# The softmax sum's small constant and broadcast move to GpSimd, and the 64-bit weight conversion takes its sign in ScalarE's pass

## The chip, the cores and the metric

The kernel runs on one core of one Trainium2 chip. The metric is the device time in microseconds (us) of one execution. The engines of the core work side by side: TensorE (PE in the profile, with its weight loads as PEld), VectorE (DVE), ScalarE (ACT), GpSimd (POOL) and SyncE (SP, which only issues transfers here).

## The reference

An attention with a bias from a small network, followed by two feed-forward stages on 2304 tokens. Cut to what matters:

```
scores = q @ k.T / 8 + bias            # 4 batches, 8 heads, 576 positions, 64 wide
attn   = exp(scores - max)
attn   = attn / (sum(attn) + 1e-9)
x      = attn @ v                      # 2304 tokens x 512
h      = x @ w_in                      # 512 -> 2048; w_in, w_out are 64-bit floats
g      = (a0 + a1 h + a2 h^2 + a3 h^3) / (1 + |b0||h| + |b1| h^2 + 1e-6)
y      = g @ w_out                     # 2048 -> 512
out    = max(y @ w1, y @ w2, y @ w3) @ w_out2   # 512 -> 768 -> 512; these weights are 64-bit too
```

## The kernel before

The kernel has three stages. In **attention** it walks over 80 units; a unit is one batch b, one tile t of 128 query rows (t = 4 is the tail of 64) and one pair p of heads, and five units (t = 0 to 4) make a block of one batch and pair. For a unit, `scores` multiplies q and k on TensorE, `reduce_min` adds the bias on VectorE and finds each row's maximum (L258), `expo` takes the exponential and its row sum on ScalarE (L264, sum into `st`), `normalise` forms the inverse sum and spreads it over 128 columns (`rb`, L269 to L272), and `transposes` turns the exponentials and `rb` on TensorE (L296, L302, L303; L303 reads `rb`). `attn_v` multiplies with v and `attn_store` applies the turned inverse sum. The transposes of a unit come two units after its scores. GpSimd splits q and k of coming pairs into a high and a low part (L138 to L153).

The **first feed-forward stage** has five blocks of tokens with 16 steps each. A step is twelve matmuls into `ph` (L459), a chain of six VectorE and five ScalarE instructions on it (`rat_poly`, `rat_inv`, `rat_newton`, L480 to L496), a split of the result `gs` by ScalarE and GpSimd (L506, L507), and two steps later twelve matmuls into `y`. The **second stage** does likewise with three products `p` and their maximum.

The weights lie in memory as 64-bit floats. `weight_stages` turns one block of 128 x 512 of them into 32-bit floats: ScalarE scales the high words (L382), VectorE shifts the low words (L383), shifts the high words and joins both (L388), takes the sign bit from the high word (L396), and then ScalarE and GpSimd split the result (L412, L413; in some blocks VectorE does L413). There are 56 such blocks: 16 of w_in during attention (`wrwin`, written back as 32-bit floats `wi_n`), 16 of the first w_out around the end of attention and the first block of feed-forward (`wrwo`), and 24 of the second stage (`wrm`, `wrmo`), of which one starts with each of the 16 steps of the last feed-forward block and the rest follow in the second stage. Three buffers (`raw`) hold the loaded words; a load waits until an earlier block has left its buffer.

SyncE follows the program's own order throughout. TensorE does too from the ninth unit to the last, and in feed-forward TensorE and VectorE do, once the last units have drained. Elsewhere a scheduler sets an engine's order when the kernel is built; on GpSimd and ScalarE it does so everywhere. Each engine carries out its list strictly in order: an instruction that has to wait holds up all behind it.

Of the kernel before, what the change touches and what calls it, by code (L numbers as in the profile page):

```python
# [12 lines left out]
AF = mybir.ActivationFunctionType  # L13
ALU = mybir.AluOpType
# [3 lines left out]
P = 128  # L18
# [10 lines left out]
TW = 1148  # L29
KN = {'NSLOT': 35, 'NRAW': 3, 'NRAWX': 2, 'NATT': 4, 'HB': 0, 'NE': 'd', 'FP': 2, 'BL': 4, 'T4': 0, 'LSP': 1, 'KX': 4, 'HT': 'ss', 'EVP': 'da', 'TTP': 'dda', 'NXS': 4, 'EARLY': 0, 'NM0': 8, 'MAN': 2, 'MANF': 3, 'A1': ['b', 'T', 'sc', 'st', 'r0', 'av', 'b', 'b', 'b', 'sq', 'n', 'r1', 'p2', 'v0', 'v1', 'e0', 'e1'], 'A2': ['sc', 'av', 'p1', 'T', 'r1', 'r0', 'n', 'st', 'p2', 'sq', 'e0', 'e1', 'v0', 'v1'], 'LL': 10, 'SL': 4, 'LL0': 9, 'SL0': 4, 'SQ': [2, 1, 1], 'CUT2': 2, 'CUT3': 3, 'WS': 9, 'WE': 70, 'WT': 61, 'XT': 8, 'XA': 3, 'XB': 8, 'F': ['g2a', 'g2d', 'h', 'g1a', 'w', 'g2p', 'g1d', 'g1p', 'y', 'x', 'g3'], 'LOW': 4, 'LOM': 3, 'LOI': 0, 'GHI': 'dve', 'GLO': 'dve', 'BED': 8, 'BE0': 16, 'NU1': 'pool', 'XE': ['act', 'pool'], 'WR': 1, 'YSP': 'act', 'LAG': 2, 'EV1': 'dve', 'XSE': 'act', 'STQ': 'sp', 'PUQ': 'sp', 'NB0': 0, 'HP': 0, 'SB': 2, 'XLA': 3, 'XLB': 6, 'XSA': 11, 'YL': 10, 'YS': 14, 'WLOW': 1}  # L30
REBIAS = 2.0 ** -112
SIGN = -(1 << 31)
QC = 1.0 + 1e-6
NSMALL = 76 + S // 4

# [2 lines left out]
def tile_attention_moe(  # L38
# [7 lines left out]
    pe, act, dve, pool, sp = nc.tensor, nc.scalar, nc.vector, nc.gpsimd, nc.sync  # L46
# [8 lines left out]
    def raw(name, shape, dt):  # L55
        return sb.tile(shape, dt, tag="raw", name=name, bufs=KN['NRAW'])
# [16 lines left out]
    def f32(ap):  # L73
        return ap.bitcast(F32)
# [11 lines left out]
    parts = (slice(TOFF - 124, TW), slice(0, TOFF - 124))  # L86
# [179 lines left out]
    def normalise(b, t, p):  # L266
        et, st = ex[b, t, p]
        r = st[:, 2:4] if t < 4 else st[:, 2:3]
        dve.tensor_scalar(r, r, 1e-9, None, ALU.add)  # L269
        rb = sb.tile([P, 2, 64], F32, tag="rb", name=f"rb{b}_{t}_{p}", bufs=4)  # L270
        dve.reciprocal(r, r)
        evac(KN["NE"], (rb, r.unsqueeze(2).to_broadcast([P, 2, 64])))  # L272
        rbs[b, t, p] = rb
        if t == 4:
            pool.tensor_copy(et[:, 1, :64], et[:, 0, 512:])
# [37 lines left out]
    def evac(e, pair):  # L313
        if e == "a":
            act.copy(*pair)
        elif e == "d":
            dve.tensor_copy(*pair)  # L317
        else:
            pool.tensor_copy(*pair)
# [32 lines left out]
    def weight_place(name, n, packed):  # L352
        if packed and len(spare) == 8:
            parts = [[spare[4 * a + k] for k in range(4)] for a in range(2)]
            spare.clear()
            wt_[name, n] = parts
            return
        wt = slot(f"w{name}{n}", [P, 9, P], F32R)
        if packed:
            spare.append(wt[:, 8])  # L360
        wt_[name, n] = wt
# [5 lines left out]
    def weight_stages(src, name, n, packed=False, lo_eng=pool, narrow=None):  # L367
        box = {}
        wide_ = src.dtype != F32

        def load():
            if wide_:
                box["r"] = raw(f"wr{name}{n}", [P, 512, 2], I32)
                sp.dma_start(box["r"], src[n].bitcast(I32).rearrange("p (c w) -> p c w", w=2))
            else:
                box["r"] = raw(f"wr{name}{n}", [P, 512], F32)
                sp.dma_start(box["r"], src[n])

        def rebias():
            if wide_:  # L380
                low, high = box["r"][:, :, 0], box["r"][:, :, 1]
                act.activation(f32(high), f32(high), AF.Copy, scale=REBIAS)  # L382
                dve.tensor_scalar(low, low, 29, None, ALU.logical_shift_right)  # L383

        def join():
            if wide_:
                low, high = box["r"][:, :, 0], box["r"][:, :, 1]
                dve.scalar_tensor_tensor(low, high, 3, low, ALU.logical_shift_left, ALU.bitwise_or)  # L388

        def sign():  # L390
            if wide_:
                low, high = box["r"][:, :, 0], box["r"][:, :, 1]
                res = low
                if narrow is not None:
                    res = sb.tile([P, 512], I32, tag="xs", name=f"wn{name}{n}", bufs=KN['NXS'])
                dve.scalar_tensor_tensor(res, high, SIGN, low, ALU.bitwise_and, ALU.bitwise_or)  # L396
                box["r"] = f32(res)

        def put():
            (act if KN["PUQ"] == "act" else sp).dma_start(narrow[n], box["r"])  # L400

        def parts():
            weight_place(name, n, packed)
            r, w = box["r"], wt_[name, n]
            if isinstance(w, list):
                for k in range(4):
                    act.copy(w[0][k], r[:, k * P:(k + 1) * P])
                for k in range(4):
                    lo_eng.tensor_tensor(w[1][k], r[:, k * P:(k + 1) * P], f32(w[0][k]), ALU.subtract)
            else:  # L410
                hi, lo = (w[:, 4 * a:4 * a + 4].rearrange("p k c -> p (k c)") for a in range(2))
                act.copy(hi, r)  # L412
                lo_eng.tensor_tensor(lo, r, f32(hi), ALU.subtract)  # L413

        if narrow is not None:
            return [load, rebias, join, lambda: (sign(), put())]
        return [load, rebias, lambda: (join(), sign()), parts]

    pipe, todo = [], []

    def weights_tick(new=1):
        for st in list(pipe):
            st.pop(0)()
            if not st:
                pipe.remove(st)
        for _ in range(new):
            if todo:
                st = weight_stages(*todo.pop(0))
                st.pop(0)()
                pipe.append(st)  # L430
# [195 lines left out]
    early = []  # L626
    if wi.dtype != F32:
        for nm, src, cnt in (("wi", wi, NF), ("wo", wo, KN['EARLY'])):
            slim[nm] = dr.tile([NF, P, 512], F32, tag=f"{nm}_n", name=f"{nm}_n")
            early += [weight_stages(src, nm + "n", f, narrow=slim[nm]) for f in range(cnt)]  # L630
    eq = [st[0] for st in early[:2]]
    for i, st in enumerate(early):
        eq += st[1:3] + [st[0] for st in early[i + 2:i + 3]] + st[3:]
    n_early = len(eq)

    def low_eng(m, f):
# [82 lines left out]
    def attn_tick(n):  # L719
# [11 lines left out]
        for step in KN["A1" if n < KN["NM0"] else "A2"]:  # L731
# [13 lines left out]
            elif step == "n" and u1:  # L745
                normalise(u1[0], u1[2], u1[3])
            elif step == "v0" and u2:
                act.copy(*ev[0])  # L748
            elif step == "v1" and u2:
                for e_ in ev[1:len(ev) - 1]:  # L750
                    evac(KN["EVP"][n % len(KN["EVP"])], e_)
                evac(KN["TTP"][n % len(KN["TTP"])], ev[-1])
            elif step == "b":
                bias_step()
            elif step in ("p1", "p2"):
                early_pop(n, 0.5 * int(step[1]))
            elif step == "av":
                if avq:
                    av, js = avq.pop(0)
                    attn_v(*av, js)  # L760
                    if 4 in js:
                        stq.append(av)
                if u2 and u2[2] == u2[1][-1]:
                    av = (u2[0], u2[1], u2[3])
                    cuts = {1: (5,), 2: (3, 2), 3: (2, 2, 1)}
                    cut = {1: (5,), 2: cuts[KN["CUT2"]], 3: cuts[KN["CUT3"]]}[len(u2[1])]
                    avq.extend((av, range(sum(cut[:k]), sum(cut[:k + 1]))) for k in range(len(cut)))
            elif step == "sq":
                for bp in splits_at.get(n, []):
                    sqq.extend(split_kq(*bp))  # L770
                for _ in range(2 if n < 10 else KN["SQ"][n % len(KN["SQ"])]):
                    if sqq:
                        sqq.pop(0)()
# [121 lines left out]
```

## Time and profile before

| what | before |
|---|---|
| median of 3 runs | 1100.29 us (1100.19 to 1100.94) |
| the profiled execution, its own time | 1100.39 us |
| its span, first to last instruction | 1098.6 us |
| busy: TensorE, VectorE, ScalarE, GpSimd | 1040.5, 750.8, 620.7, 418.9 us |
| mean granted TensorE clock | 0.985 of full speed |

Attention ends about 363 us into the span, the first feed-forward stage lies from there to about 805 us, and the second fills the rest. A busy TensorE is not one at its peak, since its records overlap; how fast it goes is read from the distance between the starts of equal groups of matmuls.

### The profile page before, as it was taken

The numbers are of one execution on the slowest core, as the hardware profiler recorded it, in microseconds if no ns is written. First come the engines' busy times: TensorE is split into PE (matmuls) and PEld (weight loads), VectorE is DVE, ScalarE is ACT, GpSimd is POOL, SyncE is SP. The second block draws the span as 40 slices with busy tenths as digits, with TensorE's granted clock in tenths as the row PEclk, the third lists the DMA queues.
The fourth block names the chain that finished last, engine by engine and source line by source line (L and its number), as shares of the span: only waits on it lengthen the run. The fifth ranks groups of instructions, "written<-read, shape, count | busy, mean of one in ns | idle before, by whom it ended". The sixth has DMA issues, their size and how long they took to land. (4 is left out here: it accounts for less than half of the span.)

```text
span 1098.6 us, 16477 instructions
## 1 busy us (share of the span) xinstructions
PE 1040.5 (95%) x5996; PEld 811.5 (74%) x5996; DVE 750.8 (68%) x1512; ACT 620.7 (57%) x1226; POOL 418.9 (38%) x409
## 2 busy tenths in 40 slices
PE   5699999999999879999999999999999999999998
PEld 2247677677776557878889788777688788888887
DVE  8496899899998899877789777799984211111111
ACT  5686667676778667766678766777632211211111
POOL 7614555455486534322233323243442330211111
PEclk9799999999999889999999999999999999999999
DMA  7486845255455422010020200223233200201010
GB/s 261 158 314 217 291 153 168 99 204 173 155 160 174 136 103 77 1 58 1 1 77 1 78 1 1 78 77 115 77 118 131 77 1 1 77 1 58 1 39 20
DMA packets 43393, 107.94 MB, mean 98 GB/s; under 512 B 4784, under 2 KB 11184, under 8 KB 43312
## 3 DMA queue, kind: packets, MB, share of 16 engines
q1 hardware_dynamic: 38128, 96.27, 26.1%
q10 hardware_dynamic: 5184, 10.62, 2.5%
q8 instruction: 47, 0.77, 0.3%
q14 instruction: 34, 0.28, 0.1%
HBM read 77.90 MB, written 28.97 MB: 97 GB/s over the span
## 5 line engine op out<-in xcount | busy, mean ns | idle before, releaser
L459 PE MATMUL p<-ys,wm 128*128 128x512 f32 (+1 forms) x1080 | 228.8, 369 | 2.8 <-POOL wm L413 1.8
L459 PE MATMUL ph<-xs,wwi 128*128 128x512 f32 (+1 forms) x960 | 217.8, 375 | 5.7 <-ACT at L748 3.5
L459 PEld LDWEIGHTS p<-ys,wm 128*128 128x128 f32 x1080 | 188.4, 188 | 39.4 <-POOL wm L413 2.2
L459 PE MATMUL y<-gs,wwo 128*128 128x512 f32 (+1 forms) x905 | 207.7, 374 | 7.9 <-POOL gs L507 7.2
L459 PEld LDWEIGHTS ph<-xs,wwi 128*128 128x128 f32 x960 | 170.4, 191 | 41.8 <-POOL xs L451 3.8
L507 POOL TENSOR_TENSOR gs<-g,gs 128x512 fp32r<-128x512 f32 (+1 forms) x80 | 102.2, 1277 | 234.6 <-ACT gs L506 160.2
L459 PEld LDWEIGHTS y<-gs,wwo 128*128 128x128 f32 x905 | 157.3, 188 | 46.4 <-POOL gs L507 13.7
L264 ACT ACTIVATE e<-e,st 128x576 f32<-128x576 f32 x144 | 111.5, 775 | 59.3 <-DVE st L258 53.4
L551 POOL TENSOR_TENSOR h2s<-mx,h2s 128x512 fp32r<-128x512 f32 (+1 forms) x30 | 35.9, 1197 | 226.9 <-ACT h2s L550 226.9
L258 DVE CUSTOM_DVE_ANT_0 e<-s,bias 128x576 f32<-128x576 f32 x144 | 104.0, 751 | 16.3 <-PE s L233 11.7
L547 DVE TENSOR_TENSOR mx<-p,mx 128x512 f32<-128x512 f32 (+1 forms) x30 | 19.1, 637 | 140.0 <-PE p L459 136.1
L480 ACT ACTIVATE s<-ph,keep 128x512 f32<-128x512 f32 (+1 forms) x80 | 49.3, 617 | 75.9 <-PE ph L459 74.1
L233 PE MATMUL s<-k,qs 128*128 128x288 f32 x512 | 86.3, 308 | 4.6 <-DVE st L258 2.8
L550 ACT CAST h2s<-mx 128x512 fp32r<-128x512 f32 (+1 forms) x30 | 17.3, 578 | 128.9 <-DVE mx L548 128.9
L296 PEld LDWEIGHTS tp<-ident,e 128*128 128x128 f32 x576 | 62.5, 142 | 35.6 <-issue 17.1
L296 PE MATMUL tp<-ident,e 128*128 128x128 f32 x576 | 82.0, 282 | 1.0 <-DVE at L317 0.8
L482 DVE SCALAR_TENSOR_TENSOR g<-g,keep,s 128x512 f32<-128x512 f32 (+1 forms) x80 | 55.2, 690 | 36.6 <-ACT g L481 36.0
L338 PE MATMUL av<-at,v 128*64 128x320 f32 (+3 forms) x576 | 77.7, 392 | 1.3 <-DVE st L269 0.7
L565 PE MATMUL o<-wmo,h2s 128*128 128x512 f32 x324 | 78.6, 390 | 0.0
L233 PEld LDWEIGHTS s<-k,qs 128*128 128x128 f32 x512 | 70.6, 189 | 9.0 <-DVE st L258 3.7
L185 PE MATMUL pb<-h,keep 128*32 128x288 f32 x576 | 48.7, 442 | 23.8 <-ACT h L173 22.6
L487 ACT ACTIVATE s<-g,keep 128x512 f32<-128x512 f32 (+1 forms) x80 | 52.7, 659 | 31.7 <-DVE g L482 31.6
(102 smaller groups left out, 1665.0 us busy)
## 6 DMA issues: line engine op xcount, KB each, us to landing
bias_d<-bo ACTq DMA_DIRECT2D x36, 288.0 KB, 2.9
kr<-in_k SPq DMA_DIRECT2D x16, 576.0 KB, 5.1
qr<-in_q SPq DMA_DIRECT2D x16, 576.0 KB, 5.6
bias<-bias_d SPq DMA_DIRECT2D x16, 576.0 KB, 5.3
wrm<-in_m SPq DMA_DIRECT2D x18, 512.0 KB, 3.6
wrwin<-in_wi SPq DMA_DIRECT2D x16, 512.0 KB, 4.4
wrwo<-in_wo SPq DMA_DIRECT2D x16, 512.0 KB, 3.7
v<-in_v SPq DMA_DIRECT2D x8, 576.0 KB, 4.5
```

The lines of the kernel that those rows point to most:

```text
L185: pe.matmul(pb[32 * c:32 * c + 32, x, :HS], lhsT=hw_sb, rhs=hs[c][:, x * HS:(x + 1) * HS], start=True, stop=True,)
L233: pe.matmul(pt[:, x, :HS], lhsT=qs[:, u, t * P:(t + 1) * P], rhs=ks[u][:, w, x * HS:(x + 1) * HS], start=w == 0, stop=w == 1,)
L258: dve.tensor_tensor_reduce(out=dst, in0=src, in1=bs, op0=ALU.add, op1=ALU.min, scale=-0.125, scalar=3.0e38, accum_out=st[:, u:u + 1],)
L264: act.activation(et[:, u], et[:, u], AF.Exp, bias=st[:, u:u + 1], scale=-1.0, accum_out=st[:, 2 + u:3 + u])
L296: pe.transpose(tp[:, j * P:(j + 1) * P], flat[:, 640 * u + j * P:640 * u + (j + 1) * P], ident)
L338: pe.matmul(po[r, :n], lhsT=l, rhs=m, start=j == 0, stop=j == 4, skip_group_check=True)
L459: pe.matmul(po, lhsT=wpart(key, a, k), rhs=rhs, start=first and i == 0, stop=last and i == 2)
L480: act.activation(s, ph, AF.Abs, scale=B0)
L482: dve.scalar_tensor_tensor(q, q, B1, s, ALU.mult, ALU.add)
L487: act.activation(s, q, AF.Ln, bias=qcol)
L507: pool.tensor_tensor(t[1], u, f32(t[0]), ALU.subtract)
L565: pe.matmul(po, lhsT=h[:, a, tt * P:(tt + 1) * P], rhs=w[c], start=j == 0 and i == 0, stop=j == NF2 - 1 and i == 2,)
```

## The change

It has two parts. In `normalise`, adding 1e-9 and spreading the inverse over `rb` are now GpSimd instructions; the reciprocal between them stays on VectorE. In `weight_stages`, ScalarE's pass over the high words is a ReLU with a slope of -2^32 for negative inputs in place of a plain scaling, so that a negative number leaves a mark which the shift in `join` moves into the sign's place; the separate VectorE pass for the sign is gone. The list of early stages is adjusted to three stages in place of four.

```
-SIGN = -(1 << 31)
+TOSIGN = -2.0 ** 32
...
     def normalise(b, t, p):
         et, st = ex[b, t, p]
         r = st[:, 2:4] if t < 4 else st[:, 2:3]
-        dve.tensor_scalar(r, r, 1e-9, None, ALU.add)
+        pool.tensor_scalar(r, r, 1e-9, 0.0, ALU.add, ALU.add)
+        dve.reciprocal(r, r)
         rb = sb.tile([P, 2, 64], F32, tag="rb", name=f"rb{b}_{t}_{p}", bufs=4)
-        dve.reciprocal(r, r)
-        evac(KN["NE"], (rb, r.unsqueeze(2).to_broadcast([P, 2, 64])))
+        pool.tensor_copy(rb, r.unsqueeze(2).to_broadcast([P, 2, 64]))
...
         def rebias():
-                act.activation(f32(high), f32(high), AF.Copy, scale=REBIAS)
+                act.activation(f32(high), f32(high), AF.Prelu, scale=REBIAS, alpha=TOSIGN)
                 dve.tensor_scalar(low, low, 29, None, ALU.logical_shift_right)
...
         def join():
-            if wide_:
-                low, high = box["r"][:, :, 0], box["r"][:, :, 1]
-                dve.scalar_tensor_tensor(low, high, 3, low, ALU.logical_shift_left, ALU.bitwise_or)
-
-        def sign():
             if wide_:
...
-                dve.scalar_tensor_tensor(res, high, SIGN, low, ALU.bitwise_and, ALU.bitwise_or)
+                dve.scalar_tensor_tensor(res, high, 3, low, ALU.logical_shift_left, ALU.bitwise_or)
...
-            return [load, rebias, join, lambda: (sign(), put())]
-        return [load, rebias, lambda: (join(), sign()), parts]
+            return [load, rebias, lambda: (join(), put())]
+        return [load, rebias, join, parts]
...
-        eq += st[1:3] + [st[0] for st in early[i + 2:i + 3]] + st[3:]
+        eq += st[1:2] + [st[0] for st in early[i + 2:i + 3]] + st[2:]
```

Order before, on GpSimd, in the third batch where the queries and keys of a coming pair are split (`qs`, `k`) while the first pair's last unit (`e_4_0`) ends:

```order
L138 TENSOR_SCALAR qs_2_2909<-qr_2_2687 128x1024
L144 TENSOR_SCALAR k_2_0_2910<-kr_2_2685 128x576
L141 TENSOR_TENSOR qs_2_2909<-qr_2_2687,qs_2_2909 64x512 x2
L275 COPY e_4_0_2872<-e_4_0_2872 128x64
L147 TENSOR_TENSOR k_2_0_2910<-kr_2_2685,k_2_0_2910 128x576
L144 TENSOR_SCALAR k_2_1_2911<-kr_2_2685 128x576
L147 TENSOR_TENSOR k_2_1_2911<-kr_2_2685,k_2_1_2911 128x576
```

And the same place with the change, where `st` is the row sum (L269 adds the constant) and `rb` the spread inverse (L272), of units t = 3, 4 and 0:

```order
L138 TENSOR_SCALAR qs_2_2900<-qr_2_2679 128x1024
L144 TENSOR_SCALAR k_2_0_2901<-kr_2_2677 128x576
L272 COPY rb_3_0_2892<-st_3_0_2822 128x128
L141 TENSOR_TENSOR qs_2_2900<-qr_2_2679,qs_2_2900 64x512 x2
L269 TENSOR_SCALAR st_4_0_2864<-st_4_0_2864 128x1
L275 COPY e_4_0_2863<-e_4_0_2863 128x64
L147 TENSOR_TENSOR k_2_0_2901<-kr_2_2677,k_2_0_2901 128x576
L144 TENSOR_SCALAR k_2_1_2902<-kr_2_2677 128x576
L269 TENSOR_SCALAR st_0_1_2916<-st_0_1_2916 128x2
L272 COPY rb_4_0_2951<-st_4_0_2864 128x128
L147 TENSOR_TENSOR k_2_1_2902<-kr_2_2677,k_2_1_2902 128x576
L272 COPY rb_0_1_2992<-st_0_1_2916 128x128
```

The additions and copies now stand between the splits, and `st_4_0` stands behind both L141.

On VectorE the reciprocal of that unit stands, with the change, behind the next unit's two bias passes (L258) and ahead of the evacuation and the bias passes that follow:

```order
L258 ISA e_0_1_2915,st_0_1_2916<-s_0_1_0_2917,bias_1_273 128x576
L258 ISA st_0_1_2916 128x1
L270 RECIPROCAL st_4_0_2864<-st_4_0_2864 128x1
L383 TENSOR_SCALAR wrwin_2663<-wrwin_2663 128x512
L317 COPY att_2_0_2772<-tt_3_0_2944 128x2x128
L258 ISA e_1_1_2964,st_1_1_2965<-s_1_1_1_2971,bias_1_432 128x576
```

Before, the addition stood at that place, the reciprocal and the copy behind it; what follows now waits there for GpSimd.

Order before, on VectorE, in the last feed-forward block, from the last instruction of one step's chain (L496) to the first of the next (L482), in a step in which VectorE also splits a weight block (L413):

```order
L496 SCALAR_TENSOR_TENSOR g_4_7874<-s_4_7873,g_4_7874 128x512
L413 TENSOR_TENSOR wm_7890<-wrm_7744,wm_7890 128x512
L388 SCALAR_TENSOR_TENSOR wrmo_7795<-wrmo_7795 128x512
L396 SCALAR_TENSOR_TENSOR wrmo_7795<-wrmo_7795 128x512
L383 TENSOR_SCALAR wrm_7846<-wrm_7846 128x512
L482 SCALAR_TENSOR_TENSOR g_5_7925<-g_5_7925,keep,s_5_7924 128x512
```

With the change (line numbers are lower by 5 there):

```order
L491 SCALAR_TENSOR_TENSOR g_4_7839<-s_4_7838,g_4_7839 128x512
L408 TENSOR_TENSOR wm_7855<-wrm_7711,wm_7855 128x512
L391 SCALAR_TENSOR_TENSOR wrmo_7761<-wrmo_7761 128x512
L383 TENSOR_SCALAR wrm_7811<-wrm_7811 128x512
L477 SCALAR_TENSOR_TENSOR g_5_7889<-g_5_7889,keep,s_5_7888 128x512
```

One of three conversion passes of the step is gone, and nothing else has moved.

## Rows read from the trace of the kernel before

**Rows 1.** The page's first part: busy us (share of the span) and instructions.

```profile
PE 1040.5 (95%) x5996; PEld 811.5 (74%) x5996; DVE 750.8 (68%) x1512; ACT 620.7 (57%) x1226; POOL 418.9 (38%) x409
```

**Rows 2.** Timeline of TensorE: start us, us, engine, line; first scores of four blocks.

```profile
124.48 1.30 PE L233 MATMUL s<-k,qs 128*128 128x288 f32 x8
...
217.01 1.30 PE L233 MATMUL s<-k,qs 128*128 128x288 f32 x8
...
234.05 1.30 PE L233 MATMUL s<-k,qs 128*128 128x288 f32 x8
...
336.75 1.30 PE L233 MATMUL s<-k,qs 128*128 128x288 f32 x8
```

**Rows 3.** Busy time by stretch, two of attention: length, PE, PEld, DVE, ACT, POOL.

```profile
217.00:234.00 17.00, 17.00 (x128) 12.64 (x127) 15.49 (x44) 12.53 (x30) 9.82 (x12) 1.00 0.59 207
...
319.00:336.00 17.00, 17.00 (x128) 12.64 (x127) 15.44 (x45) 14.42 (x37) 16.22 (x19) 1.00 0.44 126
```

**Rows 4.** VectorE's groups by form, 124 to 354 us: busy us, mean ns.

```profile
L317 DVE COPY rb<-st 128x128 f32<-128x128 f32 x65 | 30.4, 468 | 2.2
L269 DVE TENSOR_SCALAR st<-st 128x2 f32<-128x2 f32 x52 | 20.3, 391 | 0.2 <-ACT e L264 0.2
...
L269 DVE TENSOR_SCALAR st<-st 128x1 f32<-128x1 f32 x13 | 1.9, 147 | 0.0
```

**Rows 5.** Timeline of all engines around 190 us (in brackets: idle before, and releaser).

```profile
189.92 2.52 POOL L141 TENSOR_TENSOR qs<-qr,qs 64x512 fp32r<-64x512 f32 x2
...
190.10 1.18 DVE L317 COPY rb<-st 128x128 f32<-128x128 f32 x1
...
193.64 0.33 PE L302 MATMUL tt<-ident,e 128*128 128x128 f32 x1 [1.19 <-DVE at L317]
```

**Rows 6.** Two GpSimd groups: one line (ns min/median/max), and by form, 124 to 354 us.

```profile
L275 POOL COPY e<-e x16: 227/238/786, 103.8 to 354.4; 128x64 f32<-128x64 f32 x16
...
L138 POOL TENSOR_SCALAR qs<-qr 128x1024 fp32r<-128x1024 f32 x11 | 11.5, 1050 | 1.0
```

**Rows 7.** Timeline of VectorE, second bias pass of a unit that opens a block.

```profile
237.14 0.75 DVE L258 CUSTOM_DVE_ANT_0 e<-s,bias 128x576 f32<-128x576 f32 x1
```

**Rows 8.** Timeline of TensorE after attention, and one stretch's busy times (seventh value: granted clock).

```profile
367.24 5.49 PE L459 MATMUL ph<-xs,wwi 128*128 128x512 f32 x12 [3.48 <-ACT at L748]
...
389.30 1.22 PE L459 MATMUL y<-gs,wwi 128*128 128x512 f32 x2 [4.78 <-ACT gs L506]
390.32 4.56 PE L459 MATMUL ph<-xs,wwi 128*128 128x512 f32 x12
...
367.24:372.66 5.42, 5.42 (x12) 3.80 (x12) 5.36 (x10) 3.29 (x6) 0.00 (x0) 0.50 0.66 236
```

**Rows 9.** Timeline of the last feed-forward block, VectorE and then TensorE.

```profile
733.38 0.73 DVE L482 SCALAR_TENSOR_TENSOR g<-g,keep,s 128x512 f32<-128x512 f32 x1
...
738.31 0.69 DVE L396 SCALAR_TENSOR_TENSOR wrm<-wrm 128x512 int32<-128x512 int32 x1
738.92 0.42 DVE L383 TENSOR_SCALAR wrm<-wrm 128x512 int32<-128x512 int32 x1
...
752.72 0.73 DVE L482 SCALAR_TENSOR_TENSOR g<-g,keep,s 128x512 f32<-128x512 f32 x1
...
708.63 2.90 PE L459 MATMUL ph<-xs,wwi 128*128 128x512 f32 x12
...
736.26 2.90 PE L459 MATMUL ph<-xs,wwi 128*128 128x512 f32 x12
...
787.79 0.98 PE L459 MATMUL p<-ys,wm 128*128 128x512 f32 x2
```

**Rows 10.** Waits over the whole span: us in total, times, longest.

```profile
PE y L459 <- POOL gs L507: 7.2, 10, 1.2
```

**Rows 11.** ScalarE's groups by form: busy us, mean ns.

```profile
L382 ACT ACTIVATE wrm<-wrm 128x512 f32<-128x512 f32 x18 | 12.2, 679 | 15.7 <-DMA wrm<-in_m 15.7
...
L79 ACT ACT_TABLE_LOAD x1 | 1.3, 1283 | 0.7 <-PEq L885 0.7
```

## The prediction, written before the changed kernel ran

> **What bounds the kernel now.** I read the page's first part, then TensorE's starts in its timeline, then the waits that break its pace. TensorE is busy for 95% of the span, VectorE for 68%, ScalarE for 57% and GpSimd for 38% [rows 1]. Such shares are means over stages, so the pace comes first. In attention a block of five units takes 17.04 us where nothing disturbs it (217.01 to 234.05), with TensorE busy for 17.00 of 17 us [rows 2, 3]. From 124.48 to 336.75 twelve blocks take 212.27 us, and twelve at 17.04 would take 204.48 [rows 2]. So 7.8 us is all that any other engine costs there, although VectorE is busy for 15.49 of 17 us [rows 3]. The largest gain that the change can bring to attention is therefore 7.8 us, not the VectorE time that it removes.
>
> What breaks the pace in attention can be seen at 190 us. GpSimd runs two splits of q for 2.52 us, VectorE's small copy into `rb` beside them takes 1.18 us, and TensorE then waits 1.19 us for a VectorE evacuation that came late [rows 5]. The mean tells the same: that copy takes 468 ns, and the addition of 1e-9 takes 391 ns for two columns, but 147 ns for one [rows 4]. VectorE loses time to GpSimd in the very instructions that the change takes from it.
>
> After attention TensorE stands longest: 3.48 us behind a ScalarE copy, and 4.78 us behind the split of the first `gs`. Behind both waits twelve matmuls take 5.49 and 4.56 us in place of 2.90, at a granted clock of 0.50, which is 1.2 GHz, the lower of its two levels [rows 8, 9]. These three rows hold 3.48 + 4.78 + 2.59 + 1.66 = 12.5 us.
>
> In the last feed-forward block five steps took 27.63 us (708.63 to 736.26, so 5.53 a step), but the next eight took 51.53, against 44.21 at that pace: 7.3 us lost [rows 9]. VectorE sets that pace: three of its steps take 19.34 us (733.38 to 752.72), and TensorE needs 16.58 for three [rows 9].
>
> **The sign pass.** It leaves 56 times. In the last feed-forward block its place in the row is 0.61 us (738.31 to 738.92) [rows 9]. Three steps of VectorE shrink from 19.34 to 17.5 us, still 0.9 above TensorE's 16.58. Before, VectorE had fallen 3.5 us behind from 708 to 739 before TensorE waited for over a microsecond; with 0.3 us to spare in ordinary steps, it now falls behind only in each third step, the one in which it splits a weight block too, and by about 4 us in all four such rounds. I therefore leave TensorE a loss of 1.3 us and take a gain of **6** out of 7.3 (ends 5 and 7.3). In the first feed-forward block the conversions of w_out stand in the same row; TensorE's waits of `y` for `gs` are 7.2 us in all, most of them in the last block [rows 10]. I take **1** for the first block (ends 0 and 2).
>
> At the end of attention the scheduler still orders VectorE and puts conversions of w_out ahead of the first `g`. ScalarE's next copy waits for the sign pass, and TensorE for ScalarE. About eleven conversions lie there, so VectorE sheds 11 x 0.61 to 0.69, some 7 us. But the loads of w_out wait for three buffers, so a part of this only moves the stall to the load that is late next. The ends are 0 (the loads set everything) and 12.5 (both waits and the slow clock behind them go). I take **5**: about 1.5 us off each wait, and half of the 4.2 us at the lower clock.
>
> ScalarE's new pass does not stand in the trace. The nearest row is the pass that it replaces, 679 ns for the same 128x512 [rows 11]; I take the same. Its bounds are that and twice that, which would be 38 us more on an engine that idles for 43% of the span [rows 1], so nothing in the sum. Where the cover is gone, in the conversions after attention, the upper end would take back 0.7 us a conversion, which the lower end of that term covers.
>
> **The addition and the copy.** VectorE loses 30.4 + 20.3 + 1.9 = 52.6 us over 65 units, 4 us a block [rows 4], and falls from 15.5 to 11.4 of 17 us even before the sign passes. Its late evacuations should go, and with them most of the 7.8 us; I take **6** (ends 0 and 7.8).
>
> GpSimd gains two instructions a unit. A copy of 128x64 takes 0.238 us and a pass over 128x1024 takes 1.05, so 0.85 ns a column, and the copy of 128x128 is estimated at 0.29 [rows 6]. The trace has no GpSimd pass over two columns in these rows; it lies between 0 and 0.238, and I take 0.15. Together that is 0.44 us a unit, 2.2 a block. In an ordinary block 9.82 + 2.2 = 12 of 17 us fit. From 319 to 336 us, where splits of k, q and w_in meet, GpSimd is busy for 16.22 of 17 us already [rows 3], and 18.4 don't fit.
>
> The order adds a wait as well. The reciprocal now waits on VectorE for GpSimd's addition, and the next unit's evacuation and bias passes are queued behind it; ScalarE's exponentials and TensorE's scores wait for those. For t = 4 the addition stands behind `rb` of t = 3 and both L141: 0.29 + 2.52 + 0.15 = 3.0 us from one reciprocal to the next, against a unit of 17.04 / 5 = 3.41. So it just fits, and VectorE has its two bias passes to do meanwhile (0.75 each [rows 7]). From 319 to 336 us two weight splits stand between as well, and it doesn't fit. I charge **3.5** there: 1.4 of overload, and 2.1 for VectorE held behind a reciprocal (ends 0 and 8).
>
> A rule speaks against this part. The Trainium skill, GPSIMD Engine Reference, section Engine selection, recommends VectorE for elementwise work and puts GpSimd at about half its speed for two inputs, near line rate for one. At half VectorE's speed I estimate the pair at 0.8 us, which still fits the ordinary block by 0.1 us, adds 1.8 us to the overload and would make the sum 1088. The row of 0.238 us for 64 columns on GpSimd supports the faster reading.
>
> **The sum.** Against the profiled execution's 1100.39 us (span 1098.6, and 1.8 around it; the median of the runs is 1100.29): minus 6 (last block), 1 (first block), 5 (after attention) and 6 (attention), plus 3.5 (GpSimd), so minus 14.5: **1086 us**. The second stage and the start get nothing: the second stage runs on TensorE's pace, and at the start the additions only change engine.
>
> **Rivals.** *GpSimd becomes what TensorE waits for* (slower). A pair on GpSimd could cost more than 0.44 us, since it also waits for VectorE: the copy of 128x64 took up to 0.786 [rows 6]. At 2 x 0.79 = 1.58 us each of 13 blocks loses 1.58 + 2.52 - 3.41 = 0.7, the stretch at 319 us loses 16.22 + 7.9 - 17 = 7, and attention's 6 don't come: 1100.4 - 12 + 9 + 7 = 1104. It decides from about 1.35 us a pair on, where the loss eats the 12. For it speaks that GpSimd is full at 319 us; against it that VectorE issues fewer of the instructions that collide. The Trainium skill, SBUF — State Buffer, section Who interferes with whom, calls the pair of ports that both share an exclusive lock, held for the whole instruction; the trace agrees with its 1.18 us for the small copy [rows 5].
>
> *The gain after attention comes in full.* If the two waits shrink enough for the clock to stay at 2.4 GHz, 12.5 come in place of 5, and with attention's whole 7.8: about 1077. For it speaks that the lower clock appears right behind the long waits; against it the loads.
>
> *Nothing comes of it.* The loads set the pace after attention (0), attention's gain and GpSimd's loss cancel, and the last block's VectorE time returns as a wait of GpSimd's splits, whose instructions stand in the same chain: 1099 to 1101. Against it speaks that VectorE has no idle time between the steps of that block.
>
> *The new function needs another table.* Two loads a conversion at 1.283 us [rows 11] are 144 us on ScalarE, and a time well above 1110. The program of the change holds a single load, at the start, as before.
>
> **Chances.** The forecast, 1079 to 1094 by itself, gets 0.66; the full gain (1070 to 1079) 0.14; nothing 0.09; slower 0.11, the table in it. A difference under 0.2%, 2.2 us, can't be told from none here. So faster 0.80, same 0.09, slower 0.11. The range reaches from the full gain, 1072, to a gain that just shows, 1098.
>
> **What would show it.** Right: three steps near 17.5 us on VectorE in the last block and a TensorE period near 5.6; blocks of attention at 17.04 with no wait for `at` or `st` on VectorE; waits shorter than 3.48 and 4.78 after attention; GpSimd's copy near 0.29 us. Wrong: TensorE waiting for `rb`, VectorE idle ahead of reciprocals for more than a few microseconds in all, ScalarE's pass above 0.7 us, or blocks above 17.04 all through attention.

## The result, and the profile after

The changed kernel takes 1085.25 us (median of 4 runs, 1084.40 to 1086.93) against 1100.42 for the kernel before on the same chip: a ratio of 0.9863, 95% interval 0.9846 to 0.9880. The prediction was 1086.0. The profiled execution spans 1083.2 us against 1098.6, so 15.4 us less. The total was met; several of the terms were not, and that their misses cancelled was luck.

The page's first part after the change, busy us by engine, answers to [rows 1]: VectorE is shed of 93.1 us, and GpSimd takes on 33.8.

```profile
PE 1034.7 (96%) x5996; PEld 814.2 (75%) x5996; DVE 657.7 (61%) x1296; ACT 622.8 (57%) x1226; POOL 452.7 (42%) x569
```

To see where the time went I cut each span at starts that TensorE's timeline shows: the turning of `rb` (L303) of the 14th, 64th, 74th and 80th unit, the first `ph` of the second and of the last feed-forward block, the first `p`, the first `o`, and the end. "Steady attention" is the stretch from the 14th to the 64th unit. Lengths in us, from one profiled execution each:

| kernel | units to 14 | steady attention | to unit 74 | to unit 80 | first FFN block | blocks 2 to 4 | last block | to first `o` | rest |
|---|---|---|---|---|---|---|---|---|---|
| before | 128.19 | 177.71 | 34.57 | 23.01 | 101.88 | 225.83 | 96.60 | 24.78 | 286.03 |
| after | 132.24 | 170.68 | 43.25 | 21.09 | 95.07 | 225.85 | 89.28 | 21.95 | 283.79 |
| difference | +4.1 | -7.0 | +8.7 | -1.9 | -6.8 | 0 | -7.3 | -2.8 | -2.2 |

The one great loss lies in the fourth column, around 325 us, where splits of k, q and w_in meet. Busy times by stretch, as in [rows 3], of an ordinary block and of this place (the seventh value is the granted clock):

```profile
217.00:234.00 17.00, 17.00 (x128) 12.64 (x126) 13.14 (x35) 12.33 (x30) 12.46 (x23) 1.00 0.52 178
...
317.00:334.00 17.00, 12.32 (x80) 8.82 (x78) 7.13 (x23) 10.47 (x28) 15.42 (x24) 0.83 0.44 136
```

In the ordinary block TensorE has no gap, and GpSimd went from 9.82 to 12.46 of 17 us. At 317 us GpSimd is the busiest engine with 15.42, TensorE stands for 4.7, and the granted clock falls to 0.83 on average. The timeline says why. First VectorE's reciprocal of a unit with t = 4, then GpSimd's row, then TensorE:

```profile
323.83 0.16 DVE L270 RECIPROCAL st<-st 128x1 f32<-128x1 f32 x1 [2.94 <-POOL st L269]
...
323.56 0.23 POOL L269 TENSOR_SCALAR st<-st 128x1 f32<-128x1 f32 x1
323.86 0.24 POOL L275 COPY e<-e 128x64 f32<-128x64 f32 x1
324.05 1.41 POOL L147 TENSOR_TENSOR k<-kr,k 128x576 fp32r<-128x576 f32 x1
325.43 0.67 POOL L144 TENSOR_SCALAR k<-kr 128x576 fp32r<-128x576 f32 x1
326.07 1.26 POOL L408 TENSOR_TENSOR wwi<-wrwi,wwi 128x512 fp32r<-128x512 f32 x1
327.42 0.23 POOL L269 TENSOR_SCALAR st<-st 128x2 f32<-128x2 f32 x1
327.73 1.69 POOL L404 TENSOR_TENSOR wwi<-wrwi,wwi 128x128 fp32r<-128x128 f32 x4
329.36 0.29 POOL L272 COPY rb<-st 128x128 f32<-128x128 f32 x1
...
329.71 0.48 PE L303 MATMUL tt<-ident,rb 128*128 128x128 f32 x1 [4.68 <-POOL rb L272]
```

VectorE waited 2.94 us for the addition. The reciprocal ended at 323.99, but the copy, a piece of 0.29 us, started at 329.36: it stood behind 5.0 us of splits (L147, L144, L408, L404) in GpSimd's row. TensorE waited 4.68 us for it.

Over the whole column this wait and the clock behind it make up the loss. Busy times of the column before and after, then TensorE's waits in it after (total, times, longest; before it has none that the view lists):

```profile
305.90:340.47 34.57, 34.48 (x255) 25.41 (x254) 31.29 (x86) 28.43 (x69) 28.46 (x33) 1.00 0.59 185
```

```profile
302.92:346.17 43.25, 36.93 (x254) 26.82 (x253) 23.45 (x65) 30.18 (x72) 34.08 (x53) 0.92 0.50 155
...
PE tt L303 <- POOL rb L272: 6.3, 2, 4.7
```

Two waits for `rb` take 6.3 us, and the same work keeps TensorE busy for 36.93 us at a mean granted clock of 0.92 in place of 34.48 at 1.00, 2.45 us more.

### The profile page after: what moved, and what is told of

Read it like the earlier page. It is cut to its first block, busy times and chain, and to the rows that moved or that the text cites. A ratio compares the mean times of both kernels' runs of the same rounds, so it can differ in the third digit from the quotient of the medians.

```text
span 1083.2 us, 16519 instructions
## 1 busy us (share of the span) xinstructions
PE 1034.7 (96%) x5996; PEld 814.2 (75%) x5996; DVE 657.7 (61%) x1296; ACT 622.8 (57%) x1226; POOL 452.7 (42%) x569
## 5 line engine op out<-in xcount | busy, mean ns | idle before, releaser
L454 PE MATMUL y<-gs,wwo 128*128 128x512 f32 (+1 forms) x905 | 204.4, 373 | 1.3 <-POOL gs L502 1.1
L502 POOL TENSOR_TENSOR gs<-g,gs 128x512 fp32r<-128x512 f32 (+1 forms) x80 | 96.1, 1201 | 237.2 <-ACT gs L501 170.2
L258 DVE CUSTOM_DVE_ANT_0 e<-s,bias 128x576 f32<-128x576 f32 x144 | 104.3, 754 | 44.9 <-PE s L233 32.4
L560 PEld LDWEIGHTS o<-wmo,h2s 128*128 128x128 f32 x324 | 60.4, 188 | 12.6 <-POOL h2s L546 0.4
```

The source lines that it names most:

```text
L258: dve.tensor_tensor_reduce(out=dst, in0=src, in1=bs, op0=ALU.add, op1=ALU.min, scale=-0.125, scalar=3.0e38, accum_out=st[:, u:u + 1],)
L454: pe.matmul(po, lhsT=wpart(key, a, k), rhs=rhs, start=first and i == 0, stop=last and i == 2)
L502: pool.tensor_tensor(t[1], u, f32(t[0]), ALU.subtract)
L560: pe.matmul(po, lhsT=h[:, a, tt * P:(tt + 1) * P], rhs=w[c], start=j == 0 and i == 0, stop=j == NF2 - 1 and i == 2,)
```

## The experiments

All times are medians beside runs of the kernel before on the same chip. That kernel's medians there were 1097.83 to 1098.35 us (single runs 1092.8 to 1102.2), so ratios are given too. Stage lengths are in the table behind the first eight kernels. They come from one profile each: two profiles of the kernel with the new conversion alone differ by 0.5 us in steady attention (171.80 and 171.27) and by 0.7 in the first feed-forward block (91.49 and 92.23), and the one profile of the kernel before is of an execution 2.0 to 2.6 us above its medians on these chips.

**The two parts apart.** The first kernel has after's conversion with before's four lines in `normalise`, the second the reverse:

```
# new conversion only (after, with)                    # pair on GpSimd only (before, with)
-        pool.tensor_scalar(r, r, 1e-9, 0.0, ...)
+        dve.tensor_scalar(r, r, 1e-9, None, ALU.add)  -  dve.tensor_scalar(r, r, 1e-9, None, ...)
         dve.reciprocal(r, r)                          +  pool.tensor_scalar(r, r, 1e-9, 0.0, ...)
-        pool.tensor_copy(rb, ...)                     -  evac(KN["NE"], (rb, ...))
+        evac(KN["NE"], (rb, ...))                     +  pool.tensor_copy(rb, ...)
```

> Only the new conversion of the weights; the addition and the copy stay on VectorE as before. Theory (the sign pass gives the gain from the end of attention on, the GpSimd pair gives 7.0 us of steady attention and costs 4.0 at the start and 8.7 from 299 to 342 us): none of these three is left, and 6.7 + 2.0 + 7.3 + 5.1 = 21.1 us come off 1100.4, so about 1079. Rival (the losses at the start and at 299 us come from the new order of the early conversions, not from the pair): they stay, 1079 + 12.7 = 1092.

> Only the addition and the copy on GpSimd; the conversion keeps its sign pass. Theory: minus 7.0 in steady attention, plus 4.0 at the start, plus 8.7 in the crowded stretch, so about 1106. Rival (the losses belong to the conversion's new order): 1100.4 - 7.0 = 1093. Second rival (the second stage's 5.1 us come from the order of GpSimd, not from the sign pass): 1101.

The new conversion alone: 1074.47 us, ratio 0.9785 (0.9761 to 0.9810), 4.5 us better than expected, of which 2.4 are the kernel before, which is that much faster on this chip. The pair alone: 1105.56 us, ratio 1.0067 (1.0044 to 1.0089), as the theory had it. So the pair alone makes the kernel slower by 0.67%. Its losses at the start and in the fourth column are in both kernels that have it, and gone from the one that hasn't. One part of the theory fell: with the new conversion alone steady attention takes 171.80 us, 5.9 less than before, where I had expected no change. The pair alone brings it to 172.69. The stages from unit 74 to the last block gain 3.3 us more without the pair than the theory had, and the fourth column still loses 2.0 against before.

**The pair only where it doesn't hurt.** `i` is the unit's number, counted from 0:

```
-        pool.tensor_scalar(r, r, 1e-9, 0.0, ALU.add, ALU.add)
+        i = [(un[0], un[2], un[3]) for un in units].index((b, t, p))
+        if i < 15 or i >= 60:
+            dve.tensor_scalar(r, r, 1e-9, None, ALU.add)
+        else:
+            pool.tensor_scalar(r, r, 1e-9, 0.0, ALU.add, ALU.add)
...
-        pool.tensor_copy(rb, ...)
+        (dve if i < 15 or i >= 60 else pool).tensor_copy(rb, ...)
```

> As the change, but the addition and the copy go to GpSimd only for units 15 to 59; units 0 to 14 (before 124 us) and 60 to 79 (from the stretch at 299 us on) keep them on VectorE. Theory: the start's 4.0 and the stretch's 8.7 us come back, the attention blocks between stay at 17.04, so 1085.3 - 12.7 = 1072.6, below both kernels. Rival (the losses are not the pair's): 1085. Half-way (VectorE, relieved of the sign pass alone, is late in the stretch as before, 1 to 3 us): 1075.

1072.55 us (1072.23 to 1073.13), ratio 0.9771 (0.9747 to 0.9795): as the theory said. The start is back at 128.11 us and the fourth column at 36.37.

**GpSimd's row made shorter.** In the changed kernel, `'LOI': 0` becomes `'LOI': 1`, which puts the low parts of all sixteen w_in blocks on VectorE:

> As the change, but the low parts of the sixteen w_in blocks (four subtractions of 128x128 each) are formed on VectorE in place of GpSimd. Theory (GpSimd is over-full from 299 to 342 us, and the late copy into rb is what TensorE waits for): the wait of 4.68 us at 329.7 goes, the stretch falls from 43.2 to 36 us or less, and the time to 1077 to 1079. Rival (the copy is late because the pair's round trip stands behind VectorE): VectorE gets longer, the wait stays, 1085 to 1089.

1079.55 us, ratio 0.9839 (0.9814 to 0.9864). The waits of TensorE from 295 us on, to be read against the 4.68 us of the changed kernel (total, times, longest):

```profile
PE s L233 <- DVE st L258: 2.2, 1, 2.2
...
PE tt L303 <- POOL rb L272: 0.2, 1, 0.2
```

The wait for `rb` goes with the splits that stood ahead of it, and the fourth column falls from 43.25 to 38.51. Now VectorE is late once, by 2.2 us, and so the column stays above the theory's 36 and the time half a microsecond above its 1077 to 1079.

**Copy or addition.** In the changed kernel one of the two returns to VectorE:

```
# copy alone on GpSimd                                # addition alone on GpSimd
-  pool.tensor_scalar(r, r, 1e-9, 0.0, ...)           -  pool.tensor_copy(rb, ...)
+  dve.tensor_scalar(r, r, 1e-9, None, ALU.add)       +  dve.tensor_copy(rb, ...)
```

> As the change, but the addition of 1e-9 stays on VectorE; only the copy into rb is on GpSimd, so VectorE's reciprocal no longer waits for GpSimd. With the copy and addition both on VectorE the time was 1074.5, with both on GpSimd 1085.3. Theory A (GpSimd is simply over-full: what counts is its sum of 0.33 + 0.24 us a unit): the copy carries 58% of the 10.8 us, so 1080 to 1081. Theory B (the round trip counts: the reciprocal waits in VectorE's row for the addition in GpSimd's): nearly all of it goes, 1075 to 1077, and the stretch at 300 us falls from 43.2 to 37 us. Theory C (TensorE waits for the copy, wherever the addition is): 1084 to 1086.

> As the change, but the copy into rb is back on VectorE; only the addition is on GpSimd. Theory A: 42% of the 10.8 us, so 1079. Theory B: the whole loss or more, since VectorE's reciprocal still waits and the copy now stands behind it in VectorE's row: 1085 to 1088. Theory C: 1075 to 1076.

Copy alone: 1077.04 us, ratio 0.9799 (0.9783 to 0.9814). Addition alone: 1078.21, ratio 0.9811 (0.9796 to 0.9826). None of the theories holds over the whole span, and a total near one of them (B's 1077 for the copy, A's 1079 for the addition) proves nothing; by stages, C and B each hold in one. Around 325 us it is the copy (theory C): with it alone on GpSimd the fourth column is 42.00 us, with the addition alone 37.65. GpSimd's row and TensorE, copy alone:

```profile
322.29 2.51 POOL L408 TENSOR_TENSOR wwi<-wrwi,wwi 128x512 fp32r<-128x512 f32 x2
324.72 0.31 POOL L272 COPY rb<-st 128x128 f32<-128x128 f32 x1
...
325.09 0.33 PE L303 MATMUL tt<-ident,rb 128*128 128x128 f32 x1 [2.30 <-POOL rb L272]
```

This wait is half of that in the changed kernel. Another of 2.1 us, for a copy on ScalarE, and again a mean granted clock of 0.92 belong to the 42.00.

In steady attention it is the addition (theory B): that stage takes 175.19 us with the addition alone on GpSimd, 170.45 with the copy alone, and 171.80 with neither. VectorE's wait from 131 to 302 us, in the changed kernel and with the addition alone:

```profile
DVE st L270 <- POOL st L269: 3.7, 8, 1.3
```

```profile
DVE st L270 <- POOL st L269: 11.0, 14, 2.4
```

The round trip holds VectorE up for 11.0 us where it still has the copy to do as well. At the start only both together cost something: 132.24 us, against 128.33 and 128.96. In the changed kernel TensorE waits there for `rb` for 2.5 us in two waits, where it has no such wait before; what makes up the rest of the 4.1 was not found.

**Where the sign pass hurt.** On the kernel with the new conversion alone, the old pass is kept for some blocks (`names`):

```
+  if name in names: act.activation(f32(high), f32(high), AF.Copy, scale=REBIAS)
   else:             act.activation(f32(high), f32(high), AF.Prelu, scale=REBIAS, alpha=TOSIGN)
...
+  if name in names:
+      dve.scalar_tensor_tensor(low, high, 3, low, ALU.logical_shift_left, ALU.bitwise_or)
+      dve.scalar_tensor_tensor(res, high, SIGN, low, ALU.bitwise_and, ALU.bitwise_or)
```

> Addition and copy on VectorE; the sign pass on VectorE is kept (with the plain scaling on ScalarE) for the 24 blocks of the second stage alone, and gone for the 32 of w_in and w_out. Theory: the last feed-forward block takes 96.6 us again (7.3 more), and the second stage 5.0 more; all ahead of it is as without the sign pass: 1074.5 + 12.3 = 1086.8. Rival (the second stage's gain comes from another order, not from the passes): 1074.5 + 7.3 = 1081.8.

> Addition and copy on VectorE; the sign pass is kept for the 16 early blocks of w_in alone, as a second VectorE pass right behind the first, within the new list of three stages. Theory (the sixteen passes are what makes VectorE late in the steady attention blocks): attention from 128 us on takes 177.7 us again in place of 171.8, so 1074.5 + 5.9 = 1080.4. Rival (the shorter list of early stages, which comes at other places in a unit, gives it): attention stays at 172 and the time at 1074 to 1075.

Kept in the second stage's 24 blocks: 1084.21 us (1083.31 to 1087.46), ratio 0.9876 (0.9857 to 0.9894). The median lies half-way between the theory's 1086.8 and the rival's 1081.8; the stages decide. The last block takes 96.59 us again, and the second stage 24.77 + 287.65 = 312.4, against 305.8 with the new conversion alone and 310.8 before: the theory. This profile is of one of the two slowest of five executions (1086.83 us), so the size of the second stage's part is less sure. Kept in the 16 blocks of w_in: 1079.59 us, ratio 0.9825 (0.9810 to 0.9840), steady attention 178.00 us: the theory again, and the new order of the early stages is not the cause. Busy times from 131 to 302 us; the first row is the kernel before, then the new conversion alone, the pass kept for w_in, and the changed kernel (the fourth value is VectorE):

```profile
131.00:302.00 171.00, 167.53 (x1212) 123.24 (x1210) 157.08 (x439) 117.71 (x277) 88.95 (x115) 0.99 0.47 160
```

```profile
131.00:302.00 171.00, 170.31 (x1258) 126.55 (x1256) 151.96 (x434) 120.21 (x283) 91.28 (x120) 1.00 0.48 163
```

```profile
131.00:302.00 171.00, 167.82 (x1221) 123.31 (x1218) 158.57 (x435) 118.83 (x278) 91.73 (x117) 1.00 0.47 160
```

```profile
131.00:302.00 171.00, 170.98 (x1265) 126.86 (x1262) 120.59 (x336) 122.29 (x286) 121.40 (x221) 1.00 0.50 166
```

At 157 to 159 us of 171 VectorE makes TensorE stand; at 152 it hardly does any more (170.31 busy). The further 31 us that the pair takes from it buy TensorE 0.7 us. Even that isn't certain, and VectorE's busy time alone doesn't tell. Of the next two rows the first has the pair on GpSimd for units 15 to 59, with VectorE as empty and TensorE at 170.31 all the same; the second has the addition alone there:

```profile
131.00:302.00 171.00, 170.31 (x1258) 126.32 (x1256) 124.05 (x342) 121.47 (x285) 117.22 (x210) 1.00 0.50 163
```

```profile
131.00:302.00 171.00, 168.73 (x1232) 124.19 (x1232) 139.14 (x376) 118.91 (x281) 103.93 (x168) 1.00 0.49 163
```

In the second VectorE is busy for only 139 us, but it also waits 11.0 us for GpSimd, and TensorE stands for 2.3.

The stage lengths of these kernels, columns as above:

| kernel | units to 14 | steady attention | to unit 74 | to unit 80 | first FFN block | blocks 2 to 4 | last block | to first `o` | rest |
|---|---|---|---|---|---|---|---|---|---|
| new conversion alone | 128.81 | 171.80 | 36.57 | 21.45 | 91.49 | 225.77 | 89.29 | 21.95 | 283.87 |
| pair alone | 132.44 | 172.69 | 42.50 | 22.24 | 101.11 | 225.77 | 96.56 | 24.75 | 287.24 |
| pair for units 15 to 59 | 128.11 | 171.41 | 36.37 | 21.38 | 92.07 | 225.74 | 89.26 | 21.96 | 284.10 |
| after, w_in low parts on VectorE | 132.11 | 170.71 | 38.51 | 21.62 | 93.80 | 225.75 | 89.23 | 21.96 | 283.81 |
| copy alone on GpSimd | 128.33 | 170.45 | 42.00 | 21.53 | 92.78 | 225.79 | 89.27 | 21.96 | 283.99 |
| addition alone on GpSimd | 128.96 | 175.19 | 37.65 | 21.02 | 92.78 | 225.75 | 89.23 | 21.96 | 284.16 |
| sign pass kept, second stage | 127.79 | 172.62 | 36.28 | 21.45 | 92.11 | 225.74 | 96.59 | 24.77 | 287.65 |
| sign pass kept, w_in | 126.95 | 178.00 | 37.97 | 21.50 | 91.17 | 225.76 | 89.27 | 21.95 | 284.93 |

**Which version is best.** Four kernels side by side. The new ones put the copy alone on GpSimd for units 15 to 59, and, with the pair there, set `'LOI': 2`, which splits every second w_in block on VectorE:

> The new conversion alone, once more, beside the next three on one chip. 1074.5 as before, if what separates it from the mixed kernel (1072.6) is real; 1072 to 1073 if not.

> The pair on GpSimd for units 15 to 59 alone, once more. Theory (GpSimd's pair brings 0.4 us in steady attention on top of the sign pass, since one of the two is enough to keep VectorE in time): within 1 us of the kernel with the new conversion alone. Rival (the 1.9 us between the two are real): 1.5 to 2 us below it.

> Only the copy into rb on GpSimd, and only for units 15 to 59; the addition on VectorE throughout. With the copy alone on GpSimd, steady attention took 170.45 us against 171.41 with the pair in the middle and 171.80 with neither. Theory (without the round trip VectorE is never late there): 170.5 us in steady attention and 1 us less than the kernel with the pair in the middle, some 1071.5. Rival (these differences are the scatter of one profile): the same as that kernel.

> As the kernel with the pair in the middle, and every second w_in block has its low part split on VectorE in place of GpSimd. Theory (the crowded stretch from 300 us on still lies 2 us above its pace because GpSimd holds 14 to 15 of 17 us): the stretch falls from 36.4 to about 35 us, the time by 1 to 1.5. Rival (VectorE, which has the pair back there, is the next to be late): the stretch stays or grows, the time is the same or 1 to 3 us longer.

Conversion alone: 1073.58 us (1072.54 to 1075.39), ratio 0.9778 (0.9751 to 0.9805). Pair for units 15 to 59: 1072.35 (1071.07 to 1074.87), ratio 0.9765 (0.9737 to 0.9792). Copy alone there: 1072.70, ratio 0.9766 (0.9740 to 0.9792). The 1073.58 lies between its two readings, the 1.2 us to the next kernel between theory and rival, and the copy alone didn't bring the 1 us that its theory had. These three can't be told apart, with steady attention at 171.27, 171.40 and 171.15 us; a gain of 1 us or so from the pair there is not shown. With `'LOI': 2`: 1077.62, ratio 0.9807 (0.9780 to 0.9833), which is the rival's direction, but 5.3 us longer in place of 1 to 3. The fourth column grew to 38.36 us; TensorE waits there 1.2 us for VectorE and 1.3 for ScalarE. The first feed-forward block grew to 94.55, where TensorE waits once for the split of `gs`:

```profile
PE y L458 <- ACT gs L505: 3.6, 1, 3.6
```

By their ratios all three of the best beat both kernels of the change. The simplest is the new conversion alone.

## Why the prediction was right in its total, point by point

**The last block**: 6 of at most 7.3 was foretold, and 7.3 came. The reserve of 1.3 us for every third step wasn't needed. VectorE's starts, as in [rows 9]:

```profile
726.73 0.74 DVE L477 SCALAR_TENSOR_TENSOR g<-g,keep,s 128x512 f32<-128x512 f32 x1
...
739.78 0.75 DVE L489 SCALAR_TENSOR_TENSOR g<-g,keep,s 128x512 f32<-128x512 f32 x1 [0.24 <-ACT s L483]
...
743.31 0.74 DVE L477 SCALAR_TENSOR_TENSOR g<-g,keep,s 128x512 f32<-128x512 f32 x1
```

Three steps take 16.58 us, which is TensorE's own pace; VectorE even waits 0.24 us for ScalarE in a step without a weight split. My 17.5 us for three steps took off only the passes' own places in the row. In each third step of before, from 732 us on, the shift of the low words (L383) met a split of `gs` on GpSimd and took 1.51 us where it takes 0.42 elsewhere [rows 9]. Timeline of GpSimd and VectorE, before:

```profile
750.71 1.80 POOL L507 TENSOR_TENSOR gs<-g,gs 128x512 fp32r<-128x512 f32 x1 [4.34 <-DVE wrm L388]
...
751.29 1.51 DVE L383 TENSOR_SCALAR wrmo<-wrmo 128x512 int32<-128x512 int32 x1
```

After, without the pass ahead of it, the shift comes earlier. VectorE's groups by form from 726.73 to 743.31 us (busy us, mean ns):

```profile
L383 DVE TENSOR_SCALAR wrm<-wrm 128x512 int32<-128x512 int32 x3 | 1.3, 420 | 0.0
...
L383 DVE TENSOR_SCALAR wrmo<-wrmo 128x512 int32<-128x512 int32 x1 | 0.4, 423 | 0.0
```

So 19.34 - 1.83 - 1.09 = 16.4 us of row were left, less than TensorE's 16.58. The Trainium skill, SBUF — State Buffer, section Who interferes with whom, lets a VectorE shift of this kind and a GpSimd instruction exclude each other from a pair of ports; these rows agree with it.

**After attention and the first feed-forward block**: 5 + 1 foretold, 1.9 + 6.8 came. The two waits shrank to 2.64 and 2.76 us, 2.9 us less and about as foretold. Half of what the lower clock costs was to go too, and none went behind the first wait: twelve matmuls there still take 5.49 us, as in [rows 8]. The term for the first block was mis-sized: from the awaited `y` to the second block it took 76.06 us before (389.30 to 465.36) and 72.29 after (390.04 to 462.33), so 3.8 us came where the ends were 0 and 2. The changed kernel, then the kernel with the new conversion alone:

```profile
370.18 5.49 PE L454 MATMUL ph<-xs,wwi 128*128 128x512 f32 x12 [2.64 <-ACT at L743]
...
390.04 1.22 PE L454 MATMUL y<-gs,wwi 128*128 128x512 f32 x2 [2.76 <-ACT gs L501]
```

```profile
361.49 3.04 PE L454 MATMUL ph<-xs,wwi 128*128 128x512 f32 x12 [2.59 <-ACT at L743]
...
377.76 0.74 PE L454 MATMUL y<-gs,wwi 128*128 128x512 f32 x2 [1.01 <-ACT gs L501]
```

Without the pair these two stages gain 1.6 + 10.4 = 12.0 us, 11.2 in the second profile: the rival of the full gain, at 2.4 GHz behind both waits. With the pair it doesn't come; why the clock differs stays open, as told at the end.

**Attention**: 6 foretold, 7.0 came, but by another way. This is the step that failed though its number held. I gave the gain to the addition and the copy, and nothing to the sign passes of w_in, which run in the same blocks. Either part alone gets most of it: 5.9 us the conversion, 5.0 the pair. Together they get 7.0, so the pair adds 1.1 at most, with 0.5 between two profiles of the same kernel. TensorE needed VectorE to be a little less full, not by how much.

**GpSimd from 300 us on**: 3.5 foretold (0 to 8), 8.7 came, just beyond the end; 2.0 of them are lost with the new conversion alone as well. The pair costs 0.57 us, not 0.44: the copy was well estimated by its median, the addition of two columns was not, at 244 ns in place of 0.15 us. Groups by form (busy us, mean ns), and the copy's own row (ns min/median/max):

```profile
L272 POOL COPY rb<-st 128x128 f32<-128x128 f32 x80 | 26.3, 329 | 27.8 <-DVE st L270 17.2 <-PE tp L296 6.5 <-PE tt L302 2.5
...
L269 POOL TENSOR_SCALAR st<-st 128x2 f32<-128x2 f32 x64 | 15.6, 244 | 62.2 <-ACT e L264 58.8 <-DVE st L258 0.6
...
L269 POOL TENSOR_SCALAR st<-st 128x1 f32<-128x1 f32 x16 | 3.7, 233 | 1.8 <-ACT e L264 0.5
```

```profile
L272 POOL COPY rb<-st x80: 282/292/767, 64.6 to 361.4; 128x128 f32<-128x128 f32 x80
```

and the same copy on VectorE before:

```profile
L317 DVE COPY rb<-st x80: 215/228/1430, 65.7 to 357.1; 128x128 f32<-128x128 f32 x80
```

The Trainium skill, GPSIMD Engine Reference, section Engine selection, puts GpSimd near line rate for one input; the copy's median of 292 ns against VectorE's 228 for the same copy before, 1.28 times, agrees roughly. The addition to one column, 233 ns against VectorE's 147 [rows 4], is 1.6 times. The Trainium skill's advice there to use VectorE for elementwise work held, though not for the instruction's speed but for the row it stands in. The larger error was the mechanism: I charged the sum of GpSimd's work and VectorE's held reciprocal. What cost most was the copy's place behind 5.0 us of splits, with TensorE at its end, and the lower clock behind that wait. The rival "GpSimd becomes what TensorE waits for" came true in this stretch, but the gains elsewhere were larger than it allowed. The pair alone gave 1105.6. Two of the signs of being wrong came with it: TensorE waits for `rb` for 8.8 us in all, and VectorE's idle time ahead of reciprocals, for the addition, is 12.4 us.

**The start**: 0 foretold, 4.1 lost. "The additions only change engine" was wrong: the way from `st` to `rb` now goes from GpSimd to VectorE and back, and TensorE waits at its end for 2.5 us, as told above; the rest of the 4.1 stays open.

**The second stage**: 0 foretold, 5.0 gained. "The second stage runs on TensorE's pace" stood there without a row. In the trace before, TensorE's waits from 788 to 858 us were 2.6 us in all, most of them in this row, which I had not looked for (total, times, longest); after the change none is left there. The other 2.4 of the 5.0 us are in no wait that the view lists. That the sign passes are the cause is shown by the kernel that keeps them there, with 312.4 us in this stage. The row of before:

```profile
PE p L459 <- POOL wm L413: 1.8, 1, 1.8
```

**ScalarE's pass**: the same time, as foretold (a mean of 679 ns for `wrm` before [rows 11], a median of 679 now, with one table load in the span, as before):

```profile
L382 ACT ACTIVATE wrm<-wrm x18: 672/679/697, 701.9 to 825.3; 128x512 f32<-128x512 f32 x18
```

So the total was right because the misses, 4.1 + 5.2 too little loss and 1.3 + 2.7 + 1.0 + 5.0 too little gain, nearly cancel. Nothing in the working made them do so.

## What to carry to other kernels

Two edits that relieve the same engine are not worth the sum of what each is worth: price each alone at each place, and ask which of them is enough. A short instruction moved to an engine with long pieces costs what stands ahead of it in that engine's row, above all if another engine waits at its end; the busy share of GpSimd (42%) said nothing of that. Look for a part's instructions in every stage that holds them, also where the engine seems to have room.

## What the runs showed of the hardware that was not expected

GpSimd's addition over one or two columns took 233 and 244 ns (means), and its copy of 128 columns 292 (median). So nearly all of the short one's time seems not to be for its columns, as far as two operations can be compared.

The length of a wait doesn't tell the clock behind it. Twelve matmuls behind a wait of 2.6 us took 5.49 us in the changed kernel and 3.04 in the kernel with the new conversion alone. Busy times of these two stretches (seventh value the granted clock):

```profile
370.18:375.60 5.42, 5.42 (x13) 3.80 (x13) 4.86 (x10) 3.10 (x6) 0.00 (x0) 0.50 0.84 281
```

```profile
361.49:364.46 2.97, 2.97 (x12) 2.17 (x13) 2.50 (x6) 2.18 (x5) 0.00 (x0) 1.00 0.97 343
```

0.50 is 1.2 GHz, 1.00 is 2.4. With the w_in low parts on VectorE the same twelve took 4.62 us behind 2.63 us, with the pair for units 15 to 59 they took 3.04 behind 2.62. What ahead of the wait decides this stays open.
